# Batch 0's attention pairs merged in one written order, block 2 joined to blocks 0 and 1 from the fifth f pair on, and batch 2's attention later

## The chip, the cores and the metric

The kernel runs on one core of one Trainium2 chip. The metric is the device time of one launch in microseconds, the median of the runs shown. Matrix products run on TensorE (PE in the profile; its weight loads are PEld), the other work on VectorE (DVE), ScalarE (ACT) and GpSimd (POOL); DMAs are issued from SyncE's queue (SP).

## What is computed

An attention of two parts on 8 batches of 8 heads, 576 positions, 64 numbers per head, and an FFN on its output, all in float32:

```python
q_d, k_d, v_d = (mean over groups of 4 positions)          # 144 positions
out_up = repeat(softmax(0.125 * q_d @ k_d.T) @ v_d, 4)       # the far part
mask = abs(i - j) < 4
out_local = softmax(where(mask, 0.125 * q @ k.T, -1e9)) @ v  # the near part
x = (out_up + out_local) as [4608, 512]                      # tokens x model
h = x @ w_in                                                 # w_in [512, 2048]
g = s * relu(h) ** 2 + b
out = g @ w_out                                              # w_out [2048, 512]
```

The weights come as float64 (they are read as pairs of int32).

## The kernel before

**Units of work.** Two heads make a pair, so a batch has four pairs (`HP`), and a unit is one pair of one batch. Batches 0, 1 and 2 (`NE`) are done by `first_unit`: the far part by `down` (sums of four positions on VectorE, scores `sa`, softmax, transposes `tp` and `tr`, product `up`) and the near part by banded matmuls (scores `sl`, softmax in `pl`, transpose in `pt`, copies into the block-diagonal tile `bd`, product `ol`, then the sum into `x`). Batches 3 to 7 are done by `two_pairs`: `down_unit` for the far part and `local_unit`, on GpSimd and VectorE, for the near part.

**The FFN.** 4608 tokens are 18 blocks t of 256 (`TB`), the 2048 columns of `w_in` are 8 slices p of 256, called f pairs here. A step (t, p) is `gemm1` (24 matmuls: high and low parts of x and w_in, which keep float32's precision with the fast format), ReLU, square, a cast to the high part `gh` and the rest `gl`, and two or three steps later `gemm2` (12 matmuls into two PSUM banks of block t). `split_x(t)` makes the high part `xh` (ScalarE) and the low part `xl` (VectorE) of a block; it first drives the attention until the batches that the block needs are complete. Block 2 needs batches 0 and 1, block 4 batch 2.

**Weights.** `load_w(p)` loads slice p into a staging tile that will later be another slice's converted weights (`STAGE`). `split_w(p)` turns float64 bits into high and low float32 parts, in chunks of `CHUNK[p]` columns, by `convert`: one ScalarE multiply, four VectorE operations on bits, one ScalarE cast, one VectorE subtraction. Slice 7 comes in quarters through the two buffers of tag `pv`. `CONVERT_AT` says behind which step a slice is converted. `add_rows(p)` sums the rows of `w_out` on VectorE into `bias`, which `column_sums` turns into the constant that b adds.

**Order.** Instructions are issued by the program's order under priorities: a scheduler places them on each engine's queue, in order of a priority (`tc.high_priority(offset=...)`) and of what it expects to be ready. Before, the steps are: for p of 0 to 6 (`HF` = 7) blocks 0 and 1 in turn; then block 2 for p of 0 to 6; then for p = 7 blocks 0, 1 and 2; from then on one block after the other. The attention of batches 1 to 7 is one generator `gen` in small pieces, and `advance(st)` emits as many pieces behind each half step as `free` and `need` say: batch b may start at step `free[b]` and is to be through at `need[b]`. PSUM has eight banks: blocks 0, 1, 2 accumulate in banks 0 and 1, 2 and 3, 6 and 7; `gemm1` of block 1 uses bank 7 before block 2 starts, and bank 4 else; batches 1 and 2 use banks 5 and 6, then 5.

**Batch 0.** Its four pairs are emitted one after the other by `first_unit(0, hp)`, with a priority 400 ahead. Pairs 1 to 3 have tiles of their own (`make_room`; named `flat` in the profile), carved from space that weights take later, so that they can overlap. `clear(hp)` zeroes their block-diagonal tiles on GpSimd in pieces of 488 columns.

Of the kernel before, what the change touches and what calls it, by code (L numbers as in the profile page):

```python
# [62 lines left out]
def attention_ffn_kernel(ctx, tc, qk, vw_in, vr_in, vdm, qkn, vn, w_in, w_out, s_in, b_in, out):  # L63
# [40 lines left out]
    def load_pair(b, hp):  # L104
        if (b, hp) in ld:
            return
        own = {}
        if b == 0 and hp:
            room[hp] = make_room(hp)
            own = room[hp]["load"]  # L110

        def load(tag, shape, src, pool=one):
# [2 lines left out]
            return t

        tqk = load("qk", [P, 2, SP], qk[b, hp], two)
        tvr = load("vr", [P, FAC, D], vr_in[b, hp])
        tvd = load("vd", [KM, FAC, P], vdm[b, hp])
        tvw = load("vw", [P, NG, P], vw_in[HP * b + hp]) if HP * b + hp < EU else None  # L120
        ld[(b, hp)] = (tqk, tvw, tvr, tvd)
# [32 lines left out]
    nc.gpsimd.memset(omask, 0.0)  # L154
    for u in range(2):
        mu = omask[64 * u : 64 * u + 64]
        keep(mu, [[1, CH], [1, NO]], -HALO, CH)
        keep(mu, [[-1, CH], [-1, NO]], S - 1 + HALO, -CH)
# [13 lines left out]
    nc.vector.memset(db, 0.0)  # L174
# [39 lines left out]
    def convert(st, hi, lo, op, p):  # L214
# [15 lines left out]
        nc.vector.scalar_tensor_tensor(w, top, -0x80000000, w, ALU.bitwise_and, ALU.bitwise_or)  # L230
        nc.scalar.copy(hi, f)
# [36 lines left out]
    def down(b, hp, banks, tmp, dg):  # L268

        _, qc, vdr, vm = dg  # L270
        tqk, _, tvr, tvd = ld[(b, hp)]
        qt, kt = tqk[:, 0], tqk[:, 1]

        qd = tmp([P, SD], "qd")
        kd = tmp([P, SD], "kd")
        nc.vector.tensor_reduce(
            qd, qt[:, 0:S].rearrange("p (s j) -> p s j", j=FAC), AX.X, ALU.add)
        nc.vector.tensor_reduce(
            kd, kt[:, 3 : 3 + S].rearrange("p (s j) -> p s j", j=FAC), AX.X, ALU.add)
        for h in range(2):  # L280
            hs = slice(64 * h, 64 * h + 64)
            nc.scalar.copy(
# [487 lines left out]
```

## Time and profile before

| | |
|---|---|
| median of 3 runs | 971.13 us (970.21 to 973.34) |
| span of the profiled execution | 970.7 us |
| PE, DVE, ACT, POOL busy | 97%, 66%, 49%, 43% |
| read from and written to HBM | 75.63 MB, 9.44 MB |

The profiled execution is given by its span, from its first to its last instruction; a run's time is measured separately, so the two are close but not the same thing. In the profile's rows the first number is a time from the span's start in microseconds, then a duration; a group row gives a count (x), the busy time and the mean duration in nanoseconds, and after the second bar the idle time of the engine just before such instructions, with what ended it. A table of stages gives for each stretch its length and the busy time of each engine in it with the count of instructions; the last three columns are the granted TensorE clock as a share, the DMA engines' share and GB/s.

### The profile page before, as it was taken

The numbers are of one execution on the slowest core, as the hardware profiler recorded it, in microseconds if no ns is written. First come the engines' busy times: TensorE is split into PE (matmuls) and PEld (weight loads), VectorE is DVE, ScalarE is ACT, GpSimd is POOL, SyncE is SP. The second block draws the span as 40 slices with busy tenths as digits, with TensorE's granted clock in tenths as the row PEclk, the third lists the DMA queues.
The fourth block names the chain that finished last, engine by engine and source line by source line (L and its number), as shares of the span: only waits on it lengthen the run. The fifth ranks groups of instructions, "written<-read, shape, count | busy, mean of one in ns | idle before, by whom it ended". The sixth has DMA issues, their size and how long they took to land.

```text
span 970.7 us, 18541 instructions
## 1 busy us (share of the span) xinstructions
PE 938.7 (97%) x7316; PEld 843.4 (87%) x7316; DVE 637.7 (66%) x1175; ACT 475.0 (49%) x1141; POOL 418.0 (43%) x455
## 2 busy tenths in 40 slices
PE   5769999999999999999999999999999999999998
PEld 4559988888999999998888899989899999998987
DVE  5999996864567878787787878787878521211121
ACT  5878775553754453545363545453635433333231
POOL 9421011101066686776868786867676200000000
PEclk9999999999999999999999999999999999999999
DMA  9736512112243232323241424242412000000000
GB/s 316 261 121 210 172 60 78 49 42 73 101 134 113 77 110 72 102 70 133 67 136 66 135 68 131 72 134 69 136 55 76 1 22 1 23 1 22 1 23 22
DMA packets 32103, 86.26 MB, mean 89 GB/s; under 512 B 3344, under 2 KB 7952, under 8 KB 32016
## 3 DMA queue, kind: packets, MB, share of 16 engines
q1 hardware_dynamic: 32016, 85.08, 26.6%
q8 instruction: 57, 0.93, 0.4%
q14 instruction: 30, 0.25, 0.1%
HBM read 75.63 MB, written 9.44 MB: 88 GB/s over the span
## 4 chain that ended last, share of the span: by engine, by line
PE 74%; DVE 9%; DMA 8%; POOL 5%; ACT 2%; issue 2%; SPq 0%; DVEq 0%; ACTq 0%; POOLq 0%
PE ph L556 11%; PE ph L557 11%; PE ph L558 11%; PE po L603 11%; PE po L601 11%; PE po L602 11%; DMA tqk<-in_qk_dram 3%; POOL pr L466 3%; POOL acc L488 3%; DMA wst<-in_moe_w_out_dram 2%; PE sa L303 2%; DVE bias L579 1%; PE up L339 1%; PE ol L431 1%; DMA lqk<-in_qkn_dram 1%
## 5 line engine op out<-in xcount | busy, mean ns | idle before, releaser
L556 PE MATMUL ph<-xh,wi 128*128 128x256 f32 x1152 | 325.4, 283 | 3.7 <-ACT xh L542 2.5
L557 PE MATMUL ph<-xl,wi 128*128 128x256 f32 x1152 | 323.9, 281 | 0.0
L558 PE MATMUL ph<-xh,wi 128*128 128x256 f32 x1152 | 323.6, 281 | 0.0
L466 POOL TENSOR_TENSOR pr<-lqk 128x576 f32<-128x576 f32 x140 | 201.2, 1461 | 73.2 <-DMA lqk<-in_qkn_dram 29.2
L556 PEld LDWEIGHTS ph<-xh,wi 128*128 128x128 f32 x1152 | 217.5, 189 | 11.2 <-ACT xh L542 2.8
L557 PEld LDWEIGHTS ph<-xl,wi 128*128 128x128 f32 x1152 | 217.4, 189 | 5.4 <-issue 0.2
L558 PEld LDWEIGHTS ph<-xh,wi 128*128 128x128 f32 x1152 | 217.6, 189 | 0.3
L566 ACT ACTIVATE ph<-ph 128x512 f32<-128x512 f32 x144 | 83.8, 582 | 229.0 <-PE ph L558 223.2
L601 PE MATMUL po<-wo,gh 128*128 128x512 f32 x456 | 180.7, 396 | 0.0
L602 PE MATMUL po<-wo,gh 128*128 128x512 f32 x456 | 180.5, 396 | 0.0
L603 PE MATMUL po<-wo,gl 128*128 128x512 f32 x456 | 177.9, 397 | 0.0
L569 DVE TENSOR_TENSOR gl<-ph,gh 128x512 fp32r<-128x512 f32 x114 | 77.8, 683 | 115.8 <-ACT gh L568 115.5
L488 POOL TENSOR_TENSOR acc<-acc,pv 128x576 f32<-128x576 f32 x80 | 114.4, 1430 | 57.1 <-DVE acc L488 29.5
L468 DVE TENSOR_REDUCE st<-pr 128x9 f32<-128x576 f32 x140 | 105.9, 757 | 37.7 <-POOL pr L466 35.4
L292 POOL TENSOR_TENSOR dq<-vq 64x64 f32<-64x64 f32 x58 | 22.8, 393 | 197.4 <-PE up L337 195.3
L603 PEld LDWEIGHTS po<-wo,gl 128*128 128x128 f32 x456 | 85.7, 188 | 17.6 <-issue 0.2
L487 DVE TENSOR_TENSOR pv<-lv,st 128x576 f32<-128x576 f32 x120 | 87.5, 747 | 18.8 <-POOL acc L488 18.4
L601 PEld LDWEIGHTS po<-wo,gh 128*128 128x128 f32 x456 | 85.7, 188 | 15.9 <-ACT gh L568 0.6
L602 PEld LDWEIGHTS po<-wo,gh 128*128 128x128 f32 x456 | 85.7, 188 | 15.8
L568 ACT CAST gh<-ph 128x512 fp32r<-128x512 f32 x114 | 66.9, 587 | 64.3 <-PE po L602 62.4
L567 ACT ACTIVATE ph<-ph 128x512 f32<-128x512 f32 x144 | 83.7, 582 | 3.2
L602 PE MATMUL po<-wo,gb 128*128 128x512 f32 x120 | 47.1, 392 | 0.0
(149 smaller groups left out, 1239.3 us busy)
## 6 DMA issues: line engine op xcount, KB each, us to landing
tqk<-in_qk_dram SPq DMA_DIRECT2D x30, 584.0 KB, 4.1
lqk<-in_qkn_dram SPq DMA_DIRECT2D x20, 768.0 KB, 4.2
lv<-in_vn_dram SPq DMA_DIRECT2D x20, 480.0 KB, 3.4
out_dram<-os SPq DMA_DIRECT2D x17, 512.0 KB, 3.1
wst<-in_moe_w_in_dram SPq DMA_DIRECT2D x7, 1024.0 KB, 6.5
wst<-in_moe_w_out_dram SPq DMA_DIRECT2D x7, 1024.0 KB, 5.3
tvd<-in_vdm_dram SPq DMA_DIRECT2D x29, 160.0 KB, 2.9
tvr<-in_vr_dram SPq DMA_DIRECT2D x29, 128.0 KB, 3.1
```

The lines of the kernel that those rows point to most:

```text
L466: nc.gpsimd.tensor_tensor(pr, lqk[:, 0:CH], lqk[:, CH + o : 2 * CH + o], ALU.mult)
L468: nc.vector.tensor_reduce(ls[:, :, o], pr, AX.X, ALU.add)
L487: nc.vector.tensor_tensor(pv, lv[:, o : o + CH], w, ALU.mult)
L488: (nc.vector if o % 3 == 1 else nc.gpsimd).tensor_tensor(acc[:, :, h], acc[:, :, h], pv, ALU.add)
L556: nc.tensor.matmul(ph[:, j], wi[p][:, 0, k, f], xh[:, k], start=(k == 0), stop=False)
L557: nc.tensor.matmul(ph[:, j], wi[p][:, 0, k, f], xl[:, k], start=False, stop=False)
L558: nc.tensor.matmul(ph[:, j], wi[p][:, 1, k, f], xh[:, k], start=False, stop=(k == NK - 1))
L566: nc.scalar.activation(ph, ph, AF.Relu)
L567: nc.scalar.activation(ph, ph, AF.Square)
L601: nc.tensor.matmul(po[m], gh[:, j, ms], wo[p][:, 0, j], start=first, stop=False)
L602: nc.tensor.matmul(po[m], gh[:, j, ms], wo[p][:, 1, j], start=False, stop=False)
L603: nc.tensor.matmul(po[m], gl[:, j, ms], wo[p][:, 0, j], start=False, stop=last)
```

## The change

- `first_unit` is cut into three generators, which `banded` returns: `d` (far part), `v` (sums of the values), `l` (near part), each with finer pieces. For batch 0 the string `FRONT` names, piece by piece, in which order the pieces of the four pairs, of the conversion of slice 0 (`c0` to `c3`) and of the split of blocks 0 and 1 (`x`) are emitted.
- `in_order` chains the instructions emitted inside it: on each engine, each one stays behind the one before it. It holds for batch 0's front and the first pieces of pairs (1, 0) and (1, 1).
- The loads of batch 0 are ordered by kind: q and k of all pairs, then the values. The zeroing goes from GpSimd to ScalarE (pairs 1 and 2) and VectorE (pair 3). The mask of the offsets is built behind the front. Slice 0 has a staging tile of its own, so that slice 1 can be loaded ahead.
- `HF` is 4: blocks 0 and 1 take p of 0 to 3, block 2 follows with p of 0 to 3, then all three take p of 4 to 7. Block 2 starts at step 8 instead of 14. `CONVERT_AT`, `need[1]`, `free[2]` and the steps of `add_rows` move with it: batch 2's attention starts at step 24, not 16.
- `gemm1` takes banks 4 and 5 in turn for block 2 and from p = 4 on; batch 2 uses banks 2, 3 and 5.

```diff
-STAGE = (6, 6, 7, 6, 7, 6, 7)
-CONVERT_AT = (1, 2, 4, 6, 7, 8, 11)
-CHUNK = (512, 512, 512, 1024, 1024, 512, 1024)
-BEHIND = {1: 400, 2: 100, 4: 100, 5: 400}
-HF = 7
+STAGE = (7, 6, 7, 6, 7, 6, 7)
+CONVERT_AT = (0, 1, 3, 6, 9, 11, 13)
+CHUNK = (512, 512, 1024, 1024, 512, 512, 512, 256)
+HF = 4
+FRONT = (
+    "d0 l0 d0 d1 l1 d1 d0 d2 d1 d2 d0 l0 d0 v0 d2 d1 d0 d3 d1 l3 d2 v2 d1 d3 l1 l0 d2 d1 "
+    "l3 d0 l2 l0 d1 l3 d2 l2 l0 d0 l0 l2 d2 l0 c0 d2 d3 l2 v1 l3 l2 l3 d2 d3 c1 l2 d3 l1 "
+    "l0 l2 c0 d2 d1 v3 l1 d3 l0 c0 d0 d3 l2 d2 l3 c0 c1 d1 l0 c1 l1 d3 d1 l1 d0 c0 l1 l2 "
+    "d0 l3 l1 d3 d0 d2 l0 c2 c1 l2 c2 l1 l3 l0 l2 c1 l2 l0 d3 c2 l1 d1 c3 l2 l3 d3 l1 c3 "
+    "c3 l1 d3 l3 l1 x l3 x l3 x l3 c3 x c3 x c2 x x x c2 "
+)
...
-    load_pair(0, 0)
+    for hp in range(HP):
+        load_parts(0, hp, ("qk",))
+    for hp in range(HP):
+        load_parts(0, hp, ("vr", "vd"))
+    load_parts(0, 0, ("vw",))
...
-        for j in range(0, n + QV, 488):
-            nc.gpsimd.memset(da[:, j : min(j + 488, n + QV)], 0.0)
-        nc.gpsimd.memset(vm, 0.0)
+        for part in (da[:, n : n + QV], vm, da[:, 0:n]):
+            if i == 3:
+                nc.vector.memset(part, 0.0)
+            else:
+                nc.scalar.copy(part, zero.to_broadcast([P, part.shape[1]]))
...
+    def first_unit(b, hp, banks):
+
+        part = banded(b, hp, banks)
+        for steps in ("ddv", "ddd", "ll", "ll", "lll", "ddd", "ddll", "dd", "ll", "ll"):
+            with in_order() if steps == "ddv" and b == 1 and hp < 2 else contextlib.nullcontext():
+                for which in steps:
+                    next(part[which])
+            yield
...
-        ph = bank(6 if t >= 3 and p % 2 else 7 if t == 1 and p < HF else 4, [P, 2, TB], "ph")
+        if t >= 3:
+            at = (4, 6)[p % 2]
+        elif p >= HF:
+            at = (4, 5)[(3 * (p - HF) + t) % 2]
+        else:
+            at = (4, 7, (4, 5)[p % 2])[t]
+        ph = bank(at, [P, 2, TB], "ph")
...
+    def in_order():
+
+        traced = nc.cur_bb.bb.instructions
+        last = traced[-1]
+        yield
+        start = next(k for k in reversed(range(len(traced))) if traced[k] is last) + 1
+        for i in traced[start:]:
+            if i.engine in ENGINES:
+                if i.engine in tail:
+                    tc.add_manual_dep(
+                        i, tail[i.engine].name,
...
+                tail[i.engine] = i
+
+    def begin_x():
+        for t in range(2):
+            xs[t] = tuple(
+                two.tile([P, HP, TB], F32R, tag=tag, name=tag) for tag in ("xh", "xl"))
+        for hs in (slice(0, HP - 1), slice(HP - 1, HP)):
+            for t in range(2):
+                xh, xl = xs[t]
+                src = xt[0][:, hs, t * TB : t * TB + TB]
+                nc.scalar.copy(xh[:, hs], src)
+                yield
+                nc.vector.tensor_tensor(xl[:, hs], src, xh[:, hs].bitcast(F32), ALU.subtract)
+                yield
...
-    clear(1)
-    bk = banks(0, 1, 2, 3, 5, 6, 7)
+    load_w(1)
+    bk = banks(0, 1, 2, 3, 4, 5, 6, 7)
+    with tc.high_priority(offset=400):
+        with in_order():
+            nc.vector.memset(dq, 0.0)
+            for hp in range(1, HP):
+                clear(hp)
+            nc.vector.memset(db, 0.0)
+    streams = {}
     for hp in range(HP):
-        load_ahead(hp)
-        if hp > 1:
-            clear(hp)
-        with tc.high_priority(offset=400):
-            for _ in first_unit(0, hp, bk):
-                pass
-    split_w(0)
-    load_w(1)
+        for name, steps in banded(0, hp, bk).items():
+            streams[f"{name}{hp}"] = steps
+    with tc.high_priority(offset=400):
+        with in_order():
+            chunks = split_parts(0)
+            streams["x"] = begin_x()
+            for name in FRONT.split():
+                if name not in streams:
+                    streams[name] = next(chunks)
+                next(streams[name], None)
+            next(chunks, None)
+    offset_mask()
+    load_pair(*units[HP])
+    load_pair(*units[HP + 1])
     load_w(2)
-    split_x(0)
-    split_x(1)
...
-    need = [0, 2 * HF - 3] + [(S * b // TB) * NFP - 3 for b in range(2, B)]
-    free = [0, 0, 16] + [((S * (b - 1) - 1) // TB) * NFP - 2 for b in range(3, B)]
-    rings = {1: banks(5, 6), 2: banks(5), 3: banks(2, 3, 5)}
+    need = [0, 2 * HF - 1] + [(S * b // TB) * NFP - 3 for b in range(2, B)]
+    free = [0, 0, 3 * NFP] + [((S * (b - 1) - 1) // TB) * NFP - 2 for b in range(3, B)]
+    rings = {1: banks(5, 6), 2: banks(2, 3, 5)}
...
-        if 2 * HF - 1 <= st < 2 * HF - 1 + NFP:
-            add_rows((NFP - 1, *range(NFP - 1))[st - 2 * HF + 1])
+        if 0 <= st - (3 * NFP - 10) < NFP:
+            add_rows(st - (3 * NFP - 10))
```

More of the change, by code (lines that the diff above doesn't have):

```diff
@@ L102, in make_room, with load_parts, load_pair @@
                 "sm": take(pl, at + 384, [P, 2, 2 * NG])}
[L104 to L108, printed above, removed]
-            room[hp] = make_room(hp)
-            own = room[hp]["load"]
-        def load(tag, shape, src, pool=one):
+    def load_parts(b, hp, parts):
+        if b == 0 and hp and hp not in room:
+            room[hp] = make_room(hp)
+        own = room[hp]["load"] if b == 0 and hp else {}
+        got = ld.setdefault((b, hp), {})
+        for tag in parts:
+            shape, src, pool = {
+                "qk": ([P, 2, SP], qk[b, hp], two),
+                "vr": ([P, FAC, D], vr_in[b, hp], one),
+                "vd": ([KM, FAC, P], vdm[b, hp], one),
+                "vw": ([P, NG, P], vw_in[min(HP * b + hp, EU - 1)], one)}[tag]
             t = own[tag] if tag in own else pool.tile(shape, F32, tag=tag, name="t" + tag)
             nc.sync.dma_start(t, src)
[L115 to L121, printed above, removed]
-    load_pair(0, 0)
+            got[tag] = t
+    def load_pair(b, hp):
+        if (b, hp) not in ld:
+            load_parts(b, hp, ("qk", "vr", "vd") + (("vw",) if HP * b + hp < EU else ()))
+    for hp in range(HP):
[3 more added lines that the diff above has]
+    load_parts(0, 0, ("vw",))
     ident = cst.tile([P, P], F32, name="ident")
     make_identity(nc, ident)
-    load_pair(0, 1)
     mask = cst.tile([P, 3, 32], F32, name="mask")
@@ L153, in attention_ffn_kernel, with offset_mask @@
     omask = cst.tile([P, CH, NO], F32, name="omask")
[L154 to L158, printed above, removed]
+    def offset_mask():
+        nc.gpsimd.memset(omask, 0.0)
+        for u in range(2):
+            mu = omask[64 * u : 64 * u + 64]
+            keep(mu, [[1, CH], [1, NO]], -HALO, CH)
+            keep(mu, [[-1, CH], [-1, NO]], S - 1 + HALO, -CH)
     dq = cst.tile([P, NQ * 2 * GQ + 3 * P], F32, name="dq")
-    nc.vector.memset(dq, 0.0)
     QV = NQ * 2 * GQ + P
@@ L236, in split_w @@
     def split_w(p):
-        with tc.high_priority(offset=-BEHIND.get(p, 0)):
-            split_parts(p)
+        for chunk in split_parts(p):
+            for _ in chunk:
+                pass
     def split_parts(p):
@@ L266, in first, with add_values @@
         return tc.high_priority() if b >= 3 else contextlib.nullcontext()
[L268 to L282, printed above, removed]
-                qc[hs, :, GQ * h : GQ * h + GQ], qd[hs].rearrange("p (i s) -> p i s", i=NQ))
+    def add_values(b, hp, tmp, dg):
+        _, _, vdr, vm = dg
+        tvr, tvd = ld[(b, hp)]["vr"], ld[(b, hp)]["vd"]
         vt = tmp([P, 2, P], "vt")
@@ L292, in down @@
             ve.tensor_tensor(vdr[hs, hs], vq[hs, 0], vq[hs, 1], ALU.add)
+    def down(b, hp, banks, tmp, dg):
+        _, qc, vdr, vm = dg
+        tqk = ld[(b, hp)]["qk"]
+        qt, kt = tqk[:, 0], tqk[:, 1]
+        qd = tmp([P, SD], "qd")
+        kd = tmp([P, SD], "kd")
+        nc.vector.tensor_reduce(
+            qd, qt[:, 0:S].rearrange("p (s j) -> p s j", j=FAC), AX.X, ALU.add)
+        nc.vector.tensor_reduce(
+            kd, kt[:, 3 : 3 + S].rearrange("p (s j) -> p s j", j=FAC), AX.X, ALU.add)
+        yield
+        for h in range(2):
+            hs = slice(64 * h, 64 * h + 64)
+            nc.scalar.copy(
+                qc[hs, :, GQ * h : GQ * h + GQ], qd[hs].rearrange("p (i s) -> p i s", i=NQ))
         yield
@@ L342, in down, with banded @@
         return up
[L344 removed]
+    def banded(b, hp, banks):
         alt = hp if b == 0 else 0
@@ new lines, in banded, with down_unit @@
+        return {"d": far(), "v": values(), "l": near()}
+    def first_unit(b, hp, banks):
[4 more added lines that the diff above has]
+                    next(part[which])
+            yield
+    def down_unit(b, hp, banks):
+        x = new_x(b)
+        tmp = lambda shape, name: one.tile(shape, F32, tag=name, name=name)
+        dn = down(b, hp, banks, tmp, diag[0])
@@ L370, in first_unit @@
         next(dn)
+        next(dn)
+        add_values(b, hp, tmp, diag[0])
         yield
[L372 to L396 removed]
@@ L397, in first_unit @@
-        nc.scalar.activation(pl, pl, AF.Exp, scale=SCALE)
-        nc.vector.tensor_reduce(lsm, pl, AX.X, ALU.add)
-        nc.vector.tensor_scalar(lsm, lsm, 1e-9, None, ALU.add)
-        nc.vector.reciprocal(lsm, lsm)
-        (nc.vector if b else nc.gpsimd).tensor_tensor(
-            pl, pl, lsm.unsqueeze(2).to_broadcast([P, 2 * NG, 32]), ALU.mult)
-        yield
-        next(dn)
-        yield
-        next(dn)
-        if own:
-            pt = take(sc, spots["vt"], [P, 2 * NG, 32])
-        else:
-            pt = two.tile([P, 2 * NG, 32], F32, tag="pl", name="pt")
@@ L411, in first_unit @@
-        nc.vector.transpose(pt, pl)
-        for w in range(4):
-            ws = slice(32 * w, 32 * w + 32)
-            nc.scalar.copy(bd[ws, :, ws], pt[ws])
-        yield
+        for count in (3, 3, 2):
+            for _ in range(count):
+                next(dn)
+            yield
         try:
```

156 lines of the change are left out of this document (97 added, 59 removed).

## The prediction

> **What bounds the kernel now.** I read the busy table of the page, then the table of stages, then the rows of single engines that mark where a stage begins.
>
> ```profile
> span 970.7 us, 18541 instructions
> PE 938.7 (97%) x7316; PEld 843.4 (87%) x7316; DVE 637.7 (66%) x1175; ACT 475.0 (49%) x1141; POOL 418.0 (43%) x455
> ...
> 0.00:30.00 30.00, 16.84 (x324) 13.51 (x324) 18.01 (x41) 16.60 (x54) 26.79 (x69) 1.00 0.97 327
> 30.00:69.24 39.24, 28.00 (x392) 22.72 (x382) 38.01 (x87) 31.99 (x81) 10.99 (x13) 1.00 0.50 163
> 69.24:155.20 85.96, 85.96 (x879) 77.24 (x878) 79.07 (x150) 64.23 (x140) 10.66 (x18) 1.00 0.43 141
> 155.20:231.51 76.31, 74.73 (x718) 64.43 (x718) 50.35 (x98) 35.85 (x85) 7.67 (x12) 1.00 0.18 54
> 231.51:297.76 66.25, 66.07 (x611) 59.45 (x610) 40.57 (x77) 39.94 (x110) 22.53 (x30) 1.00 0.33 112
> ```
>
> A stage row gives its length, then the busy time of PE, PEld, DVE, ACT and POOL, the granted clock, the DMA share and GB/s. From 69.24 us PE has no gap, or nearly none; ahead of it lies a front in which DVE is full (38.01 of 39.24 us) and PE is not. So the time is the moment at which the FFN starts, plus TensorE's work, plus its stalls. I call a pair (t, p) of the FFN's order a step; ScalarE's ReLU (L566) marks each.
>
> ```profile
> 73.74 0.58 ACT L566 ACTIVATE ph<-ph 128x512 f32<-128x512 f32 x1 [0.52 <-PE ph L558]
> ...
> 164.96 0.58 ACT L566 ACTIVATE ph<-ph 128x512 f32<-128x512 f32 x1
> ...
> 231.51 0.58 ACT L566 ACTIVATE ph<-ph 128x512 f32<-128x512 f32 x1 [4.28 <-PE ph L558]
> ...
> 842.17 0.58 ACT L566 ACTIVATE ph<-ph 128x512 f32<-128x512 f32 x1 [2.32 <-PE ph L558]
> 886.57 0.58 ACT L566 ACTIVATE ph<-ph 128x512 f32<-128x512 f32 x1 [2.32 <-PE ph L558]
> ```
>
> The last two rows are 8 steps apart, with no attention between them: 44.40 / 8 = 5.55 us a step. The first two are 14 steps apart (91.22 us); 14 x 5.55 = 77.7, and the 13.5 left are three pairs of batch 1, whose last matmuls (L431) run from 100.23 to 153.34:
>
> ```profile
> 59.88 2.19 PE L431 MATMUL ol<-flat 128*64 128x96 f32 x24 [0.27 <-ACT flat L414]
> 67.06 2.24 PE L431 MATMUL ol<-db,tvw 128*64 128x96 f32 x24 [1.91 <-ACT db L414]
> 69.24 0.58 PE L557 MATMUL ph<-xl,wi 128*128 128x256 f32 x1
> ...
> 100.23 1.21 PE L431 MATMUL ol<-db,tvw 128*64 128x96 f32 x24
> ...
> 153.34 0.72 PE L431 MATMUL ol<-db,tvw 128*64 128x96 f32 x12
> ...
> 192.64 0.55 PE L431 MATMUL ol<-db,tvw 128*64 128x96 f32 x8
> 223.36 0.47 PE L431 MATMUL ol<-db,tvw 128*64 128x96 f32 x6
> ```
>
> So a pair costs TensorE 4.5 us in the FFN, and up to 165 us nothing is lost. From 164.96 to 231.51 there are 9 steps (49.95) and the two pairs that end at 192.64 and 223.36 (9.0): of 66.55 us, 7.6 are stall. These are steps of which all use PSUM bank 4 in `gemm1`. The row at 67.06 is the pair (1,0): before, one pair of batch 1 is already behind the FFN's start.
>
> **The change, part by part.** Time after = 970.7 - (69.24 - T) + 4.5 + (S - 7.6): T is when the FFN runs without gaps, S its stalls up to the end of batch 2, and 4.5 the pair (1,0), which now falls behind T. The steps themselves (144) and batches 3 to 7 keep their code and their due times, so they cancel.
>
> *T, the front.* `FRONT` with `in_order` puts batch 0's four pairs, the conversion of W0 and the split of x into one fixed order on each engine; batch 1's first pairs are chained behind it. What VectorE and ScalarE need for that comes from filtered tables of the stage 0 to 69.24 (tile `flat`: pairs 1 to 3 of batch 0) and 0 to 180 (tile `es`: all eight weight blocks, the sums of three stages), from the tile `bias`, and from the groups and the DMA issues:
>
> ```profile
> 0.00:69.24 69.24, 16.97 (x42) 1.00 0.70 234
> 0.00:69.24 69.24, 20.53 (x66) 1.00 0.70 234
> 0.00:69.24 69.24, 24.03 (x318) 1.00 0.70 234
> sum 180.00, DVE 90.54; mean DVE 30.18
> sum 180.00, ACT 39.91; mean ACT 13.30
> 0.00:69.24 69.24, 27.08 (x48) 1.00 0.70 234
> 155.20:231.51 76.31, 22.10 (x31) 1.00 0.18 54
> ...
> L569 DVE TENSOR_TENSOR gl<-ph,gh 128x512 fp32r<-128x512 f32 x114 | 77.8, 683 | 115.8 <-ACT gh L568 115.5
> L174 DVE MEMSET db<- 128x1536 f32 x1 | 1.3, 1338 | 0.3 <-issue 0.3
> L231 ACT CAST wo<-es 128x1024 fp32r<-128x1024 f32 x3 | 3.2, 1051 | 0.3 <-DVE es L230 0.3
> L543 DVE TENSOR_TENSOR xl<-x,xh 128x768 fp32r<-128x768 f32 x4 | 4.2, 1038 | 3.4 <-ACT xh L542 3.4
> L543 DVE TENSOR_TENSOR xl<-x,xh 128x256 fp32r<-128x256 f32 x4 | 2.3, 564 | 0.0
> ...
> tqk<-in_qk_dram SPq DMA_DIRECT2D x30, 584.0 KB, 4.1
> wst<-in_moe_w_in_dram SPq DMA_DIRECT2D x7, 1024.0 KB, 6.5
> tvd<-in_vdm_dram SPq DMA_DIRECT2D x29, 160.0 KB, 2.9
> tvr<-in_vr_dram SPq DMA_DIRECT2D x29, 128.0 KB, 3.1
> tvw<-in_vw_dram SPq DMA_DIRECT2D x9, 384.0 KB, 3.8
> ```
>
> The first three rows are DVE, ACT and PE on three pairs: 5.66, 6.84 and 8.0 us a pair. A weight block costs DVE 90.54 / 8 = 11.3 and ACT 5.0. Before the FFN's start DVE spent 27.08 us on conversion, 15.8 more than W0 alone: W1 was done ahead too. The 22.10 are the row sums. In the new front DVE has 4 x 5.66 = 22.6, W0 11.3, xl 2 x (1.04 + 0.56) = 3.2, its memsets (1.34 for 1536 columns: dq 0.6, db 1.3, `clear(3)` with 2208 columns 1.9) 3.8 and small casts 0.9: 41.8 us. ACT has 27.4 + 5.0 + about 2.5 for xh + two clears of 2208 columns at 1.05 us per 1024 (4.5): 39.4. PE has 4 x 8.0 = 32. So VectorE sets T, with ScalarE close. VectorE stood idle 30 - 18.01 + 39.24 - 38.01 = 13.2 us before 69.24, nearly all in the first 30. Bounds for T: with no idle time beyond the 1 us at the start, 43; with all 13.2, 55. All four pairs' q and k are now first in the DMA queue, the clears have left POOL's queue, where they stood between batch 0's value sums, and four pairs interleave; so I take 8 us of idle time: T = 50. W0 is behind 4 x 584 + 4 x 288 + 384 = 3.9 MB in SP's queue, and 5.9 MB at 327 GB/s end at 18 us, before VectorE gets to it; W1, vw of pairs 1 to 3 follow, none is needed sooner. The POOL work left in the front (the mask, the value sums and one product per pair) was inside 26.79 + 10.99 us with the clears, and it now has less; the mask of the offsets moves behind the front, and batch 3 is the first to read it.
>
> *S, first stretch (steps 0 to 7).* With `HF` = 4 step 8 is block 2, which needs the whole of batch 1, six steps sooner than before. VectorE must do W1, W2, W3 (33.9), four pairs with the product that POOL does in batch 0 (4 x 6.2 = 25), eight gl (0.68 each: 5.4) and xl (1.1): 65 us. TensorE has 8 x 5.55 + 4 x 4.5, less the two `gemm2` that lag (5.6), with 1.6 for a cold start: 58.4. At the density of 30 to 69 us (38.01 / 39.24) VectorE needs 67, a stall of 9; as the idle slots of the front can take a part of W1, I take 7. The bounds are 0 (they take all of the 9) and 18 (none of it, and as much again for the last pair's own chain of waits). ScalarE: 4 x 6.84 + 15 + 8 x 1.75 (ReLU, square and cast at 0.58) + 1 = 57, not the limit. W2's load waits for W0's staging, so it lands 7 us or more behind T (6.5 by its row); W2 is due at step 4, some 30 us behind T.
>
> *S, second stretch (steps 8 to 23).* No attention, 16 x 5.55 = 88.8 us of TensorE over W4 to W7 (45), the row sums (22) and gl (11): 78 us of VectorE. Two banks in turn (4 and 5) take away the cause of the 7.6. The row sums need the same number of adds; the last four need W7, whose eight quarters share a ring of two buffers, and `column_sums` on TensorE waits for them. I take 2 (0 to 6).
>
> *S, batch 2 (steps 24 to 29).* Four pairs in 5 steps, not 13. TensorE 5 x 5.55 + 18 = 46 us; ScalarE 27.4 + 8.8 = 36, VectorE 29: they fit, and x(4) is not due until step 32. ReLU and gl queue behind attention: 3 (0 to 8).
>
> S = 7 + 2 + 3 = 12. Time = 970.7 - 19.2 + 4.5 + 4.4 = 960.4 of span; the profiled run's span is 0.4 us under the median of the runs, so 961.
>
> **A rule beside a row.** TensorE runs at half pace in the front, though the granted clock is 1.00 in those stages:
>
> ```profile
> 70.04 0.41 PE L557 MATMUL ph<-xl,wi 128*128 128x256 f32 x1
> 70.26 0.41 PE L558 MATMUL ph<-xh,wi 128*128 128x256 f32 x1
> ...
> 73.07 0.28 PE L558 MATMUL ph<-xh,wi 128*128 128x256 f32 x1
> 73.19 0.28 PE L556 MATMUL ph<-xh,wi 128*128 128x256 f32 x1
> ```
>
> The same matmul starts every 0.22 us at 70 and every 0.12 us at 73; L431's 24 take 2.19 us at 60 and 1.21 at 100. The gapless run began at 69.24, so half pace costs 3 us of it by half: the 1.6 above. The Trainium skill, "TensorE: Matmul & The Clock Gate", Part 1, says that the array is slow until it has been busy for one window of about 3.4 us, and slow again after an idle window as long. The trace agrees on the warming; by that rule stalls over 3.4 us in steps 0 to 7 would each add a cold start, which the third rival prices.
>
> **Rivals.** *A denser front.* If four interleaved pairs keep PE busy without gaps, it warms up there: a pair falls from 8.0 to 4.5 us of PE, waits between the engines shorten, and idle time falls to 3: T = 46, S = 8: 952. For it: VectorE was 97% full from 30 to 69 us. Against it: PE was cold there too, with 28.00 of 39.24 busy.
>
> *What was done ahead is only paid later.* Before, W1 (11.3) and pair (1,0) lay in the front. If VectorE has no slack to do them beside steps 0 to 7, T gains but S takes it: T = 52, S = 18: 970.7 - 17.2 + 4.5 + 10.4 = 968.4, and to 973 with T = 56. For it: 65 us of VectorE against 58.4 of TensorE.
>
> *Slower: block 2 starves.* The fixed order meets waits other than it was written for, and pairs of batch 1, emitted in half the steps, have their matmuls stand in PE's queue ahead of `gemm1`: PE waits, cools, and pays 1.6 us per restart. It decides from T + S = 72.3 on. T = 54 with S = 24 (three stalls over 3.4 us, each with its 1.6, on top of the 12) gives 976.4.
>
> **Chances.** A difference under 0.3% (2.9 us) can't be told from none. Forecast (954 to 967.5) 0.50; denser front (under 954) 0.17; paid later 0.16, mostly within 0.3%; slower 0.17. Faster 0.69, same 0.14, slower 0.17. The range goes from T = 46 with S = 6 (950) to T = 55 with S = 23 (976.5) and leaves out about 2 in 10.
>
> **What would show it.** Right: first gapless `gemm1` at 46 to 55 us; DVE idle before it 6 to 10 us; W1 converted after it; step 8's ReLU near 124 us (before: step 8 at 121, but with two pairs of batch 1 less); steps 8 to 23 5.6 to 5.8 us apart; four `ol` groups of batch 2 within 60 us. Wrong: PE gaps between steps 2 and 8 over 12 us in sum, a wait of `cs` on the row sums, ReLUs of steps 24 to 31 that wait for ScalarE's attention, or T beyond 56.

## The result and the profile after

The changed kernel takes 1033.18 us (1031.71 to 1035.12, four runs) against 972.24 for the kernel before (970.21 to 973.65, four runs): a ratio of 1.0627 [1.0606, 1.0647], 6% slower. The profiled execution of the changed kernel has a span of 1031.6 us, 60.9 more than before.

From the page after: the span, the busy table, and of the 40 slices the rows of PE and of the granted clock.

```profile
span 1031.6 us, 18544 instructions
PE 951.5 (92%) x7316; PEld 854.7 (83%) x7316; DVE 643.6 (62%) x1188; ACT 480.7 (47%) x1153; POOL 418.8 (41%) x440
...
PE   5879546999998899979999999999999999999998
...
PEclk8599756999998899989999999999999999999999
```

No engine has notably more work (PE 12.8 us, DVE 5.9, ACT 5.7). What came is idle time of PE, most of it in slices 5 to 7 (103 to 181 us). The ReLU of each step (now L627) dates it; from the timeline after, steps 0, 1, 2, 7, 8, 24, 31, 32, 47 and 48:

```profile
56.93 0.57 ACT L627 ACTIVATE ph<-ph 128x512 f32<-128x512 f32 x1
58.63 0.59 ACT L627 ACTIVATE ph<-ph 128x512 f32<-128x512 f32 x1
74.67 0.58 ACT L627 ACTIVATE ph<-ph 128x512 f32<-128x512 f32 x1
...
104.20 0.58 ACT L627 ACTIVATE ph<-ph 128x512 f32<-128x512 f32 x1 [0.51 <-PE ph L619]
175.59 0.58 ACT L627 ACTIVATE ph<-ph 128x512 f32<-128x512 f32 x1 [1.15 <-PE ph L619]
...
259.21 0.58 ACT L627 ACTIVATE ph<-ph 128x512 f32<-128x512 f32 x1 [2.42 <-PE ph L619]
...
310.82 0.58 ACT L627 ACTIVATE ph<-ph 128x512 f32<-128x512 f32 x1 [0.51 <-PE ph L619]
346.83 0.59 ACT L627 ACTIVATE ph<-ph 128x512 f32<-128x512 f32 x1
...
434.51 0.58 ACT L627 ACTIVATE ph<-ph 128x512 f32<-128x512 f32 x1
458.25 0.57 ACT L627 ACTIVATE ph<-ph 128x512 f32<-128x512 f32 x1
```

Step 0 comes 16.8 us sooner than before (73.74). Then four steps come long after the one ahead of them, from ReLU to ReLU, which is what a wait at a step means below: 16.0 us at step 2 (W1), 71.4 at step 8 (block 2 waits for batch 1), 36.0 at step 32 (block 4 waits for batch 2), 23.7 at step 48 (batch 3). Before, the same four steps follow the last after 5.5, 6.1, 3.7 and 7.5 us. Steps 31 and 32 of the kernel before, which the sums below need (the row at 260.17 us in that view is two steps in one):

```profile
284.99 0.59 ACT L566 ACTIVATE ph<-ph 128x512 f32<-128x512 f32 x1
288.68 0.61 ACT L566 ACTIVATE ph<-ph 128x512 f32<-128x512 f32 x1
```

The stage table after, cut at those steps (length, busy PE, PEld, DVE, ACT, POOL, granted clock, DMA share, GB/s):

```profile
0.00:52.50 52.50, 36.26 (x628) 31.76 (x629) 44.77 (x95) 41.44 (x110) 24.95 (x60) 0.71 0.84 281
52.50:104.20 51.70, 43.92 (x382) 38.16 (x382) 48.59 (x86) 33.97 (x74) 4.92 (x6) 0.96 0.40 134
104.20:175.60 71.40, 36.89 (x428) 30.05 (x427) 62.22 (x133) 36.21 (x89) 12.57 (x18) 0.62 0.32 101
175.60:259.20 83.60, 83.60 (x552) 76.59 (x552) 22.75 (x42) 31.77 (x58) 0.00 (x0) 1.00 0.04 12
259.20:310.80 51.60, 50.19 (x627) 44.23 (x626) 23.62 (x50) 28.80 (x78) 4.66 (x12) 1.00 0.25 82
310.80:346.80 36.00, 28.92 (x276) 24.54 (x276) 17.11 (x36) 18.35 (x53) 8.64 (x15) 0.81 0.35 112
```

In the long wait VectorE is 87% busy and PE half. In the stretch behind it PE has no gap, and VectorE, which was to convert W4 to W7 there, has 22.75 us of work: it did the rest ahead. The row sums are one part of it; their group of VectorE from 50 to 160 us (count, then busy time and mean ns):

```profile
L640 DVE TENSOR_TENSOR bias<-bias,wo 128x512 f32<-128x512 f32 x26 | 17.9, 689 | 0.0
```

L640 adds row sums, due from step 14 on; 26 of them run before step 8. By tile, conversion takes 65.08 us of VectorE between the ReLUs of steps 0 and 8, where W1 to W3 are 33.9 at most:

```profile
56.90:104.20 47.30, 29.03 (x45) 0.96 0.42 139
104.20:175.60 71.40, 36.05 (x71) 0.62 0.32 101
sum 118.70, DVE 65.08; mean DVE 32.54
```

How this filler stands in VectorE's queue is seen in the timeline after, beside the first row sum of the kernel before in a fence of its own:

```profile
54.69 0.68 DVE L638 TENSOR_TENSOR bias<-wo 128x512 f32<-128x512 f32 x1
...
57.48 0.74 DVE L308 TENSOR_REDUCE qd<-tqk 128x144 f32<-128x576 f32 x1
58.15 0.68 DVE L640 TENSOR_TENSOR bias<-bias,wo 128x512 f32<-128x512 f32 x1
...
61.40 0.74 DVE L310 TENSOR_REDUCE kd<-tqk 128x144 f32<-128x576 f32 x1
```

```profile
176.96 0.68 DVE L577 TENSOR_TENSOR bias<-wo 128x512 f32<-128x512 f32 x1
```

A row sum that step 14 emits runs 2 us ahead of the first ReLU, and the next one stands between the two reductions (L308, L310) with which a pair of batch 1 begins. Before, the chain of these adds began with slice 7, which is converted last, so none could run before 177 us. The change begins it with slice 0, ready at the end of the front, and drops `BEHIND`, the lower priority of slices 1, 2, 4 and 5.

The last rows concern the pairs: the sums into `x` that end batch 1's four and batch 2's four, from the timeline after.

```profile
94.77 0.81 DVE L466 TENSOR_TENSOR x<-ol,ups 128x288 f32<-128x288 f32 x2
127.26 0.45 DVE L466 TENSOR_TENSOR x<-ol,ups 128x288 f32<-128x288 f32 x1
...
148.85 0.46 DVE L466 TENSOR_TENSOR x<-ol,ups 128x288 f32<-128x288 f32 x1
...
167.92 0.81 DVE L466 TENSOR_TENSOR x<-ol,ups 128x288 f32<-128x288 f32 x2
...
286.88 0.82 DVE L466 TENSOR_TENSOR x<-ol,ups 128x288 f32<-128x288 f32 x2 [5.14 <-PE ol L462]
305.68 0.82 DVE L466 TENSOR_TENSOR x<-ol,ups 128x288 f32<-128x288 f32 x2 [0.25 <-PE ol L462]
322.81 0.82 DVE L466 TENSOR_TENSOR x<-ol,ups 128x288 f32<-128x288 f32 x2 [6.69 <-PE ol L462]
338.76 0.79 DVE L466 TENSOR_TENSOR x<-ol,ups 128x288 f32<-128x288 f32 x2
```

Batch 2's pairs end 16 to 19 us apart, though a pair has 4.5 us of PE's time, 5.66 of VectorE's and 6.84 of ScalarE's, and VectorE and ScalarE are half idle there.

### The profile page after: what moved, and what is told of

Its sections match the earlier page's. It is cut to its first block, busy times and chain, and to the rows that moved or that the text cites. A ratio compares the mean times of both kernels' runs of the same rounds, so it can differ in the third digit from the quotient of the medians.

```text
span 1031.6 us, 18544 instructions
## 1 busy us (share of the span) xinstructions
PE 951.5 (92%) x7316; PEld 854.7 (83%) x7316; DVE 643.6 (62%) x1188; ACT 480.7 (47%) x1153; POOL 418.8 (41%) x440
## 4 chain that ended last, share of the span: by engine, by line
PE 63%; DVE 13%; POOL 10%; DMA 7%; ACT 3%; issue 3%; DVEq 0%; POOLq 0%; SPq 0%; ACTq 0%
PE ph L617 10%; PE ph L618 10%; PE ph L619 9%; PE po L663 9%; PE po L664 9%; PE po L662 9%; POOL pr L521 6%; POOL acc L543 3%; DMA tqk<-in_qk_dram 3%; DMA lqk<-in_qkn_dram 3%; PE sa L327 2%; DVE es L244 1%; DVE st L523 1%; DMA wst<-in_moe_w_in_dram 1%; DVE pv L542 1%
## 5 line engine op out<-in xcount | busy, mean ns | idle before, releaser
L521 POOL TENSOR_TENSOR pr<-lqk 128x576 f32<-128x576 f32 x140 | 206.6, 1501 | 84.9 <-DMA lqk<-in_qkn_dram 62.1
L617 PEld LDWEIGHTS ph<-xh,wi 128*128 128x128 f32 x1152 | 221.0, 192 | 11.8 <-DVE gl L630 3.4
L618 PEld LDWEIGHTS ph<-xl,wi 128*128 128x128 f32 x1152 | 220.6, 192 | 5.4 <-DVE xl L598 0.5
L619 PEld LDWEIGHTS ph<-xh,wi 128*128 128x128 f32 x1152 | 221.0, 192 | 0.1
L627 ACT ACTIVATE ph<-ph 128x512 f32<-128x512 f32 x144 | 83.7, 581 | 219.3 <-PE ph L619 218.4
L542 DVE TENSOR_TENSOR pv<-lv,st 128x576 f32<-128x576 f32 x120 | 87.3, 748 | 23.1 <-POOL acc L543 22.3
L629 ACT CAST gh<-ph 128x512 fp32r<-128x512 f32 x114 | 66.6, 585 | 74.9 <-PE po L663 72.4
## 6 DMA issues: line engine op xcount, KB each, us to landing
tvr<-in_vr_dram SPq DMA_DIRECT2D x29, 128.0 KB, 2.3
```

Of the source, the lines that this page charges most:

```text
L521: nc.gpsimd.tensor_tensor(pr, lqk[:, 0:CH], lqk[:, CH + o : 2 * CH + o], ALU.mult)
L542: nc.vector.tensor_tensor(pv, lv[:, o : o + CH], w, ALU.mult)
L617: nc.tensor.matmul(ph[:, j], wi[p][:, 0, k, f], xh[:, k], start=(k == 0), stop=False)
L618: nc.tensor.matmul(ph[:, j], wi[p][:, 0, k, f], xl[:, k], start=False, stop=False)
L619: nc.tensor.matmul(ph[:, j], wi[p][:, 1, k, f], xh[:, k], start=False, stop=(k == NK - 1))
L627: nc.scalar.activation(ph, ph, AF.Relu)
```

## The experiments

All ratios are to the kernel before, run on the same chip beside it (medians of 971.2 to 972.5 us).

**Halves of the change.** First the front alone: the new front with the old steps, `HF`, `BEHIND`, banks and due times.

```diff
-HF = 4
+HF = 7
+BEHIND = {1: 400, 2: 100, 4: 100, 5: 400}
-    free = [0, 0, 3 * NFP]
+    free = [0, 0, 16]
...
```

> The changed front alone: the written order, its loads and clears, with the steps of before (seven f pairs ahead of block 2, the old due times, banks and conversion steps, row sums from slice 7, conversions of slices 1, 2, 4, 5 with lower priority). If the prediction's term for the front is right (FFN starts at 52 us, not 69, less 4.5 us for pair (1,0)) and slice 1 can be converted beside the first steps: 956 to 964 us. If what lay in the front is only paid later: 968 to 975.

981.08 us, 1.0099 [1.008, 1.0117]. Step 0 comes at 54.3 us (before 73.74), step 13 at 145.0 (158.0), and then block 2 waits; ReLUs of steps 13 and 14 and the stage between them, of this kernel:

```profile
144.99 0.58 ACT L624 ACTIVATE ph<-ph 128x512 f32<-128x512 f32 x1
176.81 0.58 ACT L624 ACTIVATE ph<-ph 128x512 f32<-128x512 f32 x1 [0.90 <-PE ph L616]
```

```profile
145.00:176.80 31.80, 22.01 (x225) 18.53 (x223) 19.52 (x51) 15.38 (x47) 2.42 (x6) 0.73 0.30 97
```

The 19 us that the front gains are spent on a wait for batch 1, whose last pair ends at 169.7 us (before 154.7), and 10 more. No engine is full in that wait. Batch 1's pairs end at 89.1, 119.8, 150.9 and 169.7 us (before 70.7, 101.6, 130.0, 154.7): beside running steps they come 25 to 31 us apart in both kernels, and here the first one, no longer done ahead, starts the series 18 us later. The FFN's earlier start does not bring batch 1 forward, and the time lies above both ranges.

Then the steps alone: the front of before with the changed steps.

```diff
-HF = 7
-BEHIND = {1: 400, 2: 100, 4: 100, 5: 400}
+HF = 4
-    need = [0, 2 * HF - 3]
+    need = [0, 2 * HF - 1]
-    free = [0, 0, 16]
+    free = [0, 0, 3 * NFP]
...
```

> The other half of the change alone: the front of before (pairs one after the other, slice 1 and pair (1,0) done inside it), with the changed steps (block 2 from the fifth f pair on, conversion steps, banks, due times, row sums from slice 0, no lowered priorities). If the steps are the cause: 1015 to 1045 us, step 8 at 165 or later, waits at 32 and 48 as in the changed kernel. If the front is the cause, or only the two together: under 990 us.

1027.75 us, 1.0578 [1.0547, 1.061]: the steps alone cost 56 us. Step 0 comes at 77.4 us and step 8 at 175.3, the same moment as with the new front (175.6); steps 32 and 48 wait 33.7 and 25.3 us.

Is the front's loss due to `in_order` on batch 1's first pieces? The front alone, without it:

```diff
-            with in_order() if steps == "ddv" and b == 1 and hp < 2 else contextlib.nullcontext():
+            with contextlib.nullcontext():
```

> The changed front with the steps of before (that took 981 us, with 32 us between the ReLUs of steps 13 and 14), and batch 1's first pieces no longer chained behind the front. If that chain makes pair (1, 0) late (its last product at 83 us, against 67 in the kernel before) and with it the rest of batch 1: it comes 5 to 12 us sooner, the wait at step 14 shrinks by as much, 970 to 976 us. If VectorE's order in steps 0 to 13 sets the later pairs' pace of 30 us: (1, 3) ends at 165 or later as before and the time stays at 978 to 984.

982.2 us, 1.0101 [1.0077, 1.0125]. Pair (1, 0) ends 8 us sooner (81.4), the last pair of batch 1 at 169.1 against 169.7, step 14 at 175.3 against 176.8. The chaining is not the cause: the later pairs (118.0, 150.3 and 169.1) lose the 8 us again. What sets their pace this run does not show.

**The filler on VectorE.** The order of the row sums, once put back in the changed kernel, once changed in the old one:

```diff
-            add_rows(st - (3 * NFP - 10))
+            add_rows((NFP - 1, *range(NFP - 1))[st - (3 * NFP - 10)])
-        if p == 0:
+        if p == NFP - 1:
```

> The changed kernel with one part undone: the row sums start with slice 7, as before, so that their chain of adds can't begin until slice 7 is converted. Theory 1 (VectorE is filled with work that is not due: 27 row sums, 16.5 us, and slices 4 to 6, some 29 us, stand ahead of batch 1's pairs): x of block 2 comes 16 us sooner, step 8's ReLU at 155 to 162 us instead of 175.6, the time 1012 to 1022 us. Theory 2 (the pairs of batch 1 follow each other through single buffers, 17 us or more each, whatever VectorE does): step 8 stays at 170 or later and the time at 1028 or more.

1025.75 us, 1.0559 [1.0528, 1.0589]: step 8 comes at 169.6 instead of 175.6, the waits at steps 32 and 48 stay (36.3 and 26.3). Step and time lie between the two theories.

```diff
-            add_rows((NFP - 1, *range(NFP - 1))[st - 2 * HF + 1])
+            add_rows(st - 2 * HF + 1)
-        if p == NFP - 1:
+        if p == 0:
```

> The kernel before with one edit: the row sums start with slice 0 instead of slice 7. Theory 1: the adds (31 of 0.6 us) move forward into the stretch from 65 to 155 us, in which VectorE was 92% busy, and TensorE then waits there: 975 to 990 us. Theory 2: VectorE's surplus is not what matters, the time stays within 0.3% of 972.

982.58 us, 1.0114 [1.0084, 1.0145]. In the old kernel that one order is worth 11 us: beginning with slice 7 looks arbitrary, and it is what holds the adds back. In the changed kernel it gives 7: conversion stays as large between steps 0 and 8 (67.77 us of VectorE; 65.08 in the changed kernel). So both were held: the row sums in the old order, and the VectorE work of slices 4 to 7 put behind block 2's split; then, with the new order of row sums, both put behind that split.

```diff
-CONVERT_AT = (0, 1, 3, 6, 9, 11, 13)
+CONVERT_AT = (0, 1, 3, 8, 9, 11, 13)
...
+        if p >= 4:
...
+                if i.engine == nc.vector.engine:
+                    tc.add_manual_dep(
+                        i, mark[0].name,
...
```

`mark` holds the last VectorE instruction of block 2's split.

> The changed kernel with VectorE's early filler held back: row sums from slice 7 on, and the VectorE instructions of slices 4 to 7 chained behind the split of block 2 (slice 4 emitted at step 8 instead of 6). Theory 1: batch 1 ends at about 52 + 70 us, step 8's ReLU at 125 to 135 us, and the 40 to 50 us are gained: 983 to 993 us, with the waits at steps 32 and 48 left. Theory 2: four pairs of 17 to 22 us one after another end at 140 or later, step 8 at 145 to 160: 1003 to 1018 us.

1023.46 us, 1.0532 [1.0503, 1.0562]: step 8 comes at 148.6, 27 us sooner and in theory 2's range, but step 27 follows step 26 after 20.0 us, and step 32 waits 36.9. The row sums now run last, up to 250 us, with VectorE full (7.49 of the 7.80 us from 241.2 to 249.0); `column_sums` comes behind them, and the outputs of the first blocks need it. Its own matmul waits only 1.2 us for the last sum, so this is not one wait of 20 us.

```diff
-CONVERT_AT = (0, 1, 3, 6, 9, 11, 13)
+CONVERT_AT = (0, 1, 3, 8, 9, 11, 13)
...
-            add_rows(st - (3 * NFP - 10))
+            with held():
+                add_rows(st - (3 * NFP - 10))
...
-            split_w(at_step[st])
+            with held():
+                split_w(at_step[st])
```

> The changed kernel with VectorE's instructions of the row sums and of the conversion of slices 4 to 7 chained behind the split of block 2, the row sums from slice 0 as in the change. Batch 1 has VectorE to itself, without the wait of the column sums that the run with slice 7 first had at step 27. Theory L: step 8's ReLU at 145 to 150 us, 26 to 30 us sooner than in the changed kernel, the waits at 32 and 48 unchanged: 1002 to 1010 us. If the filler was the whole cause: step 8 at 130 or sooner and under 990 us.

1007.58 us, 1.0375 [1.0349, 1.0402], 25.6 less than the changed kernel (by the ratios 24.5), as theory L has it. Step 8 comes at 147.4; batch 1's pairs end at 90.9, 112.8, 125.6 and 140.9 us. The wait ahead of step 8 is still 44.6 us, and VectorE is no longer what fills it; the stage of this kernel:

```profile
104.00:147.40 43.40, 29.78 (x371) 24.75 (x370) 21.15 (x46) 18.26 (x54) 7.10 (x18) 0.72 0.27 81
```

21.15 of 43.40 us where there were 62.22 of 71.40. The filler's price is shown by taking it away: some 26 us net. The held work comes back behind step 8, where steps 8 to 24 take 91.1 us instead of 83.6.

**Batch 2 and the rest.** Batch 2 as early as before (step 16), on bank 5 alone, with the old bank rule of `gemm1`; first in the changed kernel, then with the filler held.

```diff
-    free = [0, 0, 3 * NFP]
+    free = [0, 0, 16]
-    rings = {1: banks(5, 6), 2: banks(2, 3, 5)}
+    rings = {1: banks(5, 6), 2: banks(5), 3: banks(2, 3, 5)}
+        at = 6 if t >= 3 and p % 2 else 7 if t == 1 and p < HF else 4
...
```

> The changed kernel with batch 2's part of the change undone: its attention may start at step 16 again, on bank 5 (the last two pairs on 2, 3, 5), and gemm1 uses bank 4 alone (7 for block 1 ahead of block 2), as before. Theory L (four pairs follow one another at 15 to 17 us, so 72 us from step 24 on, where TensorE has work for 46): the waits at step 32 (36 us from ReLU to ReLU) and 48 (24 us) fall to under 12 each, 40 us in sum, and the single bank costs up to 8: 993 to 1003 us. Theory F (only VectorE's early filler ahead of block 2 matters): step 8 stays at 175 and the time at 1025 or more.

1018.88 us, 1.0492 [1.0466, 1.0517]. The waits at steps 32 and 48 are gone (3.8 and 7.5 us as in the kernel before; 36.0 and 23.7 in the changed kernel), but batch 2's work now lies in steps 8 to 24, which take 108.8 us instead of 83.6. From step 24 to 32 it is 50.4 instead of 87.6, from there to the end 679.8 instead of 684.8; step 8 comes 1.8 later. By spans 15 us remain (25.2 - 37.2 - 5.0 + 1.8 = -15.2), so the time lies between the two theories.

Both together:

```diff
+            with held():
                 add_rows(st - (3 * NFP - 10))
...
-    free = [0, 0, 3 * NFP]
+    free = [0, 0, 16]
...
```

> Both: row sums and slices 4 to 7 held back, batch 2 from step 16 with the old banks. Theory L: the two gains add, 27 and 30 to 40: 964 to 980 us, about as before. Theory F: as with the hold alone, 1002 us or more.

998.29 us, 1.0277 [1.0256, 1.0298]: the two remedies together give 35 of the 61 us, more than either alone (25.6 and 14.3) and less than their sum; neither theory's range has the time. What is left over the kernel before is all there at step 24 (264.15 against 238.41, 25.7 us) and does not grow (314.44 against 288.68 at step 32). Two stages of this kernel, ahead of step 8 and behind it:

```profile
110.00:145.00 35.00, 23.11 (x330) 19.15 (x329) 16.40 (x38) 15.71 (x48) 7.08 (x18) 0.59 0.31 95
145.00:180.00 35.00, 29.73 (x257) 25.24 (x257) 35.00 (x70) 20.47 (x45) 9.03 (x6) 0.84 0.25 84
```

Ahead of step 8 no engine is full; behind it VectorE is, with the work that was held. Two more kernels vary this one. In the first, block 2 joins two pairs later:

```diff
-CONVERT_AT = (0, 1, 3, 8, 9, 11, 13)
-HF = 4
+CONVERT_AT = (0, 1, 3, 5, 7, 12, 13)
+HF = 6
-    need = [0, 2 * HF - 1]
+    need = [0, 2 * HF - 4]
...
```

> The changed front with block 2 from the seventh f pair on (HF 6: step 12), row sums and slices 6 and 7 held behind the split of block 2, batch 2 from step 16 with the old banks. Theory L (batch 1's four pairs end at 141 to 150 us at best, whatever stands in the steps): 12 steps of TensorE end near 135, so the wait ahead of block 2 shrinks from 35 to 5 to 15 us, and the time falls to 962 to 976 us. If the wait follows from VectorE's load alone (slices 1 to 5, four pairs: 90 us from 52 on), step 12 is at 155 or later and the time 978 to 990.

995.32 us, 1.0254 [1.0231, 1.0277]: the wait moves to step 12 (128.0 to 163.4), where batch 1's last sum is at 157.6. That is late enough for the theory of VectorE's load, but the time is above both ranges. VectorE is busy for 64.95 of the 71.60 us from step 0 to step 11, the pairs come 30.0, 20.6 and 15.6 us apart (91.4, 121.4, 142.0, 157.6), and the last two end in the wait, where VectorE has 16.02 of 35.40 us. So beside running steps VectorE's load stays a suspect. In the second, `gemm1` keeps the change's banks 4 and 5 in turn, with batch 2 on bank 5:

```diff
-        at = 6 if t >= 3 and p % 2 else 7 if t == 1 and p < HF else 4
+        if t >= 3:
+            at = (4, 6)[p % 2]
+        elif p >= HF:
+            at = (4, 5)[(3 * (p - HF) + t) % 2]
+        else:
+            at = (4, 7, (4, 5)[p % 2])[t]
```

> The kernel with row sums and slices 4 to 7 held and batch 2 from step 16 on bank 5, but gemm1 takes banks 4 and 5 in turn as in the change. With bank 4 alone and all else the same it took 998 us, 116 us from step 8 to 24. If the single bank made that stretch long: 8 to 24 in 100 to 106 us and 984 to 992 us. If VectorE's held work and batch 2's pairs did, or sharing bank 5 costs as much: 996 us or more.

1027.94 us, 1.058 [1.0556, 1.0604]: sharing bank 5 between `gemm1` and batch 2 loses 30 us against the one with bank 4 alone.

**What paces the pairs.** Two suspects on top of the held filler: the ring of PSUM banks (a third bank for batch 1, blocks 0 and 1 of `gemm1` on bank 4), and what is left of VectorE's load (the four bit operations of slices 1 to 3 left out).

```diff
-            at = (4, 7, (4, 5)[p % 2])[t]
+            at = (4, 4, (4, 5)[p % 2])[t]
-    rings = {1: banks(5, 6), 2: banks(2, 3, 5)}
+    rings = {1: banks(5, 6, 7), 2: banks(2, 3, 5)}
```

> The kernel with both held back, and a third PSUM bank for batch 1: banks 5, 6, 7, gemm1 of blocks 0 and 1 on bank 4 alone. If the two banks in turn (eight tiles a pair) are what sets 15 us a pair, the pairs come at 12 us or less and step 8 at 136 to 142 us (hold alone: about 148), the time 8 to 12 us under the hold alone. If the pair's own chain of waits sets it, or gemm1's single bank costs as much: within 3 us of the hold alone, or slower.

1001.15 us, 1.0309 [1.0282, 1.0337]. The first pair ends 9 us sooner (81.7), the others 21.4, 14.8 and 16.5 us after one another; step 8 comes at 140.2, as the theory of the ring has it, but the pairs are no closer (21.9, 12.8 and 15.3 us with the hold alone), and the gain of 6.4 us lies between the two forecasts. A third bank did not quicken the pairs; `gemm1`'s single bank was changed with it and slowed the steps (step 7 at 135.7 us instead of 102.8), so the ring is not tested by itself.

```diff
+        if p not in (1, 2, 3):
             nc.vector.tensor_scalar(f, f, W_MAX, -W_MAX, ALU.min, ALU.max)
             ...
```

> The kernel with row sums and slices 4 to 7 held back, and besides VectorE's four bit operations left out of the conversion of slices 1 to 3 (so these slices are not the float64's values; about 25 us of VectorE less ahead of block 2). It parts the wait that holding back left at step 8 (147 us) into VectorE's load and the pairs' own chain. If the chain of pairs sets it (first pair 20 to 25 us after 53, then 15 each): the pairs end at 75, 90, 105, 120 us and step 8 comes at 125 to 130, still 10 us or more behind TensorE's own work (115). If the load sets it: pairs under 12 us each, step 8 at 113 to 118. If neither: above 138.

1006.7 us (one run), step 8 at 145.1 us against 147.4, outside both theories' ranges: behind step 7 this load is not it either. The first pair comes 7 us sooner (83.7), the others 22.3, 15.9 and 15.6 us after one another, no closer than with the hold alone. Stages of this kernel, and the score and `ol` matmuls of its last pairs from PE's timeline:

```profile
60.00:110.00 50.00, 50.00 (x468) 43.59 (x467) 19.56 (x40) 31.06 (x74) 4.68 (x12) 0.97 0.32 111
110.00:120.00 10.00, 4.30 (x113) 3.19 (x111) 5.52 (x13) 6.55 (x22) 2.35 (x6) 0.73 0.39 114
120.00:130.00 10.00, 6.69 (x135) 5.47 (x135) 4.89 (x13) 5.21 (x18) 0.00 (x0) 0.67 0.37 110
130.00:140.00 10.00, 5.00 (x33) 4.06 (x34) 3.64 (x8) 3.14 (x6) 2.35 (x6) 0.50 0.24 78
```

```profile
108.69 0.72 PE L479 MATMUL ol<-db,tvw 128*64 128x96 f32 x12
109.34 0.98 PE L344 MATMUL sa<-kd,dq 128*96 128x144 f32 x6
...
120.48 2.19 PE L479 MATMUL ol<-db,tvw 128*64 128x96 f32 x24 [3.16 <-ACT db L469]
122.59 1.76 PE L344 MATMUL sa<-kd,dq 128*96 128x144 f32 x6
...
135.08 2.24 PE L479 MATMUL ol<-db,tvw 128*64 128x96 f32 x24 [3.37 <-ACT db L469]
```

To 110 us PE is full: the eight steps run at full speed and only two of the four pairs get done beside them. Then the pairs stand alone, strictly one behind the other: the next pair's first matmul (`sa`) follows the last of the pair before (`ol`), and from `sa` to `ol` it takes 11 to 12.5 us with every engine at 7 tenths or less.

## Why the prediction was wrong, point by point

**T was right in size.** `gemm1` of step 0 runs at full pace from 53 us on; the forecast was 50, between 43 and 55. Up to 52.5 us VectorE is busy for 44.77 us (41.8 in the sum) and idle for 7.7 (8). "W1 converted after it" held too, but "the FFN runs without gaps" from there did not: steps 0 and 1 need W0 alone and come 1.7 us apart, and step 2 waits 16.0 us for W1, whose operations share VectorE's queue with row sums and batch 1. "A denser front" did not come: PE was busy for 36.26 of the 52.5 us, with a granted clock of 0.71.

**S is the step that failed.** By the prediction's own sizes of a step and a pair:

| stretch | took | TensorE's own | stall | forecast |
|---|---|---|---|---|
| steps 0 to 7 and the wait at 8 | 118.7 | 8 x 5.55 + 18 = 62.4 | 56.3 | 7 (0 to 18) |
| steps 8 to 23 | 83.6 | 88.8 | -5.2 | 2 (0 to 6) |
| steps 24 to 31 and the wait at 32 | 87.6 | 62.4 | 25.2 | 3 (0 to 8) |

That is S = 76.3 instead of 12. The same count gives 5.8 for the kernel before (214.9 us from step 0 to step 32, of which 32 x 5.55 + 7 x 4.5 = 209.1), near the 7.6 that the prediction took from steps 14 to 23. Behind step 32 another 2.8 us came (684.8 us to the end against 682.0), where the prediction had batches 3 to 7 cancel. The sum is -16.8 + 4.5 + 76.3 - 5.8 + 2.8 = 61.0, within rounding the 60.9 by which the spans differ.

*First stretch.* "VectorE needs 65 us" listed what the eight steps need, and took for granted that VectorE would do no more there. It did: between the ReLUs of steps 0 and 8 VectorE is busy for 107 us, as row sums and slices 4 to 6 ran ahead of batch 1's work. The queue was laid out by what was expected ready and not by what block 2 waits for. That is some 26 us of the 61 (held: 1007.58). The line "the row sums need the same number of adds" looked at their number and missed that their order set when they could begin; in the old kernel that alone is 11 us.

*The other error of the same line* is that four pairs were priced by engine sums (25 us of VectorE, 18 of TensorE). With the filler held the stretch still takes 90.5 us (147.37 - 56.85) against 62.4 of TensorE, a stall of 28 where the upper bound was 18. The pairs go in series. From step 0's ReLU to the sum into `x` of batch 1's last pair it takes 111 us in the changed kernel, 84 with the filler held, 80 with VectorE relieved as well, against 62 of TensorE for steps and pairs together. The kernel before covers that series with 14 steps and has one pair done ahead; the front alone shows that even 14 steps are too few without that pair. With the filler held and batch 2 early, 26 us remain, and the two stages of that kernel's trace above place them ahead of step 8 (no engine full) and just behind it (the held work).

*Batch 2.* "They fit" is the same error: 36 us of ScalarE in 46 of TensorE, but four pairs 16 to 19 us apart end at 339.6, and block 4 waits. Started as early as before, the wait at 32 falls from 36.0 to 3.8.

*Batches 3 to 7.* The wait at step 48 had no term; it is 16.3 us longer than before (23.7 against 7.5). In the sum it counts for little, as steps 32 to 47 and what follows step 48 run 13.5 us faster than before. The first products of batch 3's near part on GpSimd come 68 us later than before; timelines after, then before:

```profile
342.85 4.17 POOL L521 TENSOR_TENSOR pr<-lqk 128x576 f32<-128x576 f32 x3 [10.25 <-DMA lqk<-in_qkn_dram]
```

```profile
274.72 9.72 POOL L466 TENSOR_TENSOR pr<-lqk 128x576 f32<-128x576 f32 x7 [4.20 <-DMA lqk<-in_qkn_dram]
```

`gen` is one generator, so batch 3's pieces follow batch 2's, also on an engine that batch 2 hardly uses. With batch 2 early the wait falls from 23.7 to 7.5 us, as before.

**The second stretch has no stall, as forecast**: 5.23 us a step, with two banks in turn, and under the 5.6 to 5.8 that were to show it. Luck has a part in that, as VectorE had done its work ahead: the stretch took back 5 of the 56 us, and with that work held it takes 91.1 us (5.7 a step). That the single bank was the cause of the 7.6 was not tested by itself.

**The rivals.** "What was done ahead is only paid later" is what the front alone does: T gained 19 us, a wait ahead of block 2 took 32, and 981.08 us is 8 us above the upper end it was given. "Block 2 starves" has the right place and sign. Its price was three cold restarts and some queueing, S = 24; it did not ask how long four pairs take one after the other. The sign that was to show the forecast wrong, "PE gaps between steps 2 and 8 over 12 us in sum", is in the trace with 34.5 us between steps 7 and 8 alone (71.40 - 36.89).

**Open.** What holds the pairs in series is not settled. A third bank (with `gemm1` on one) and a lighter VectorE left their pace in the wait; beside running steps VectorE's load was not parted from the rest. That PE's queue has the next pair's scores behind the `ol` of the pair before is seen, but no run changed it. How much of the 12 us of such a pair is PE at half pace was not separated either: its 24 `ol` matmuls take 2.19 us at 120 us, where before they took 1.21. The Trainium skill, "TensorE: Matmul & The Clock Gate", Part 1, has the array slow again after an idle window as long as the one of 3.4 us that warms it. In the trace with VectorE relieved no such window was needed: the granted clock falls to half at 114.55 us, though the longest gap of PE from 105 us to there is 1.53 us. PE's busy time and the granted clock on both sides of the fall:

```profile
111.14:114.55 3.41, 1.27 (x55) 1.00 0.38 112
114.55:124.79 10.24, 6.39 (x66) 0.50 0.35 107
```

So several short gaps in a row were enough, and a count of stalls over 3.4 us, as in the third rival, can miss cold starts.

## What to carry to other kernels

When a join is moved forward, price it by how long the chain of what it waits for takes (length of a unit times units in series), not by what those units need of each engine: here four pairs with 18 us of TensorE took 80 us beside eight steps with 44, and a front that starts the rest sooner gains nothing while the join's chain ends when it did. Before an odd order or a lowered priority is straightened out, ask what it holds back: on an engine that runs its queue in order, work that is ready but not due stands ahead of work that is due. Dependencies that held it behind the join gave back 26 us, but the held work then had to fit somewhere else.
